# Small groups in one piece, halves crossed by ways, and another order of the first last slot: a gated-attention and mixer kernel on one core

## The chip, the cores and the metric

The kernel runs on one core of a Trainium2 chip. The metric is the time of one execution on the device in microseconds; the times quoted are of single executions or the median of several. The engines are TensorE (PE; its weight loads are PEld), VectorE (DVE), ScalarE (ACT), GpSimd (POOL) and SyncE (SP), which issues all DMAs here. Each takes its instructions in order and waits on semaphores.

## The reference, cut to what matters

Eight batches, each with 3136 positions of 256 values:

```
scores = z @ z.T / 3136;  x = u * (relu(scores)**2 @ v)      # attention, gated
h = (x.T @ U @ V).T                                          # rank 32, mixes positions
y = x + h
out = y + relu(y @ w_ch1) @ w_ch2                            # 256 -> 1024 -> 256
```

## The kernel before, in words

**Tiles.** The 3136 positions of a batch are cut into seven groups: six of 512 and a small one of 64. An item is a batch and a group; there are 56, and a slot of the main loop does the attention of one item, the (x + h) unit of the item seven slots back, the first layer (w_ch1) of the item eight back and the second layer (w_ch2) of that same item. So the small groups of batches 0 to 5 come to their first layer in the slots whose attention is of group 0 of batches 2 to 7. After the main loop come seven more slots without attention (the loop over `k` at the end of the kernel, below called the last slots): slot k does the first layer of group k of the last batch beside the second layer of the group before, and the small groups of the last two batches fall into k = 0 and k = 5. The last of these slots has a second layer only, done in two halves of 256 positions (`ch2_halves`).

**Row halves and ways.** All large matmuls use half of the array's rows (64), and `pair` issues two at a time, one for each half of the rows, into different banks of one PSUM buffer of two banks. In way 0 the upper half of the rows writes bank 0 and the lower half bank 1; in way 1 they are crossed. Both ways together give the full sum over 128 rows. A bank may be written by the other half of the rows only when the first has done with it: `post` (L168) puts a signal on GpSimd that waits for the last matmul of a way, and the first weight load of the next way waits for GpSimd. Between the two ways other work is placed where there is some. `Ways` makes the units of a long accumulation, all of one way and then all of the other.

**PSUM.** There are four such buffers. `take_ps` hands out the one that a running estimate says is free first; the matmul that first writes it waits for the engine that read its old content.

**First layer.** `ch1_part` computes two of the eight blocks of 128 hidden values for all positions of a group, in one way; `parts` lists the eight calls of an item. After way 1 the result is rectified out of PSUM into a block, by VectorE (L903) or ScalarE (L906), whichever the estimate says is free first. For a small group each call is two pairs with 64 columns, and each of its four PSUM buffers is rectified by an instruction of 128x128 elements. `by_pair` orders the calls of a small group in the last slots so that way 1 follows way 0 of the same two blocks.

**Second layer.** `ch2_stream` accumulates it over the hidden values in both ways; `ch2_out` adds (x + h) (L980) and stores. For a small group `ch2_small` (L994) uses four tiles of the array, and `four_sums` (L680, L682, L684) and L980 add up. `ch2_halves` makes two `Ways` in two PSUM buffers, one for each half; its adds are L966 and its stores L967.

**(x + h).** `u2_unit` multiplies V and t1 (t1 = x.T U, made by `t1_all`: L742, then L754, L755 and a copy to the lower rows, L756), adds x on VectorE (L815), casts the sum to bf16 (L198 on ScalarE or L200 on VectorE) and turns it by a DMA transpose (L730) into `u2T`, the input of the first layer. For group 0 of the last batch, `u2T_unit` makes the turned sum directly (L859) from an x that was turned earlier; its plain sum is made by `u2_unit` with turn=False.

**Order.** `emit` runs a list of light units (pairs of a long accumulation) and puts units from queues between them: each entry has a place (an index in the light units), the number of PSUM buffers that should be free, and the unit. The places are written by hand. Other matmuls seen in the profile are the scores (zzT; evicted by L358 on ScalarE or L354 on VectorE, squared by L348) and the attention (v_bf).

Of the kernel before, what the change touches and what calls it, by code (L numbers as in the profile page):

```python
# [10 lines left out]
AF = mybir.ActivationFunctionType  # L11
# [7 lines left out]
def kernel(  # L19
# [11 lines left out]
    nc = tc.nc  # L31
# [52 lines left out]
    def take_block():  # L84
        k = free_blocks.pop(0)
        return k, pool.tile([P, GT, GW], BF16, name=f"blk{k}", bufs=1)
# [77 lines left out]
    def post(k):  # L164

        last = [wrote[k, bank] for bank in range(2) if (k, bank) in wrote]
        if any(e[2] is None for e in last):
            x = nc.gpsimd.nop(nofuse=True)  # L168
            for e in last:
                behind(x, e[1])  # L170
                e[2] = x
# [163 lines left out]
    def flat_of(entry):  # L335
        return entry[1].rearrange("p a c -> p (a c)")
# [529 lines left out]
    def ch1_part(b, g, h0, way, box):  # L866
# [37 lines left out]
        else:  # L904
            ps_free[k] = book("act", ready, 9.5 * gw / GW)
            nc.scalar.activation(out=r, in_=ps[:, :, :gw], func=AF.Relu)  # L906

    def ch2_stream(b, g, box):
        def step(i, way, first, least):
            if first:  # L910
                box["k"], box["ps"] = take_ps()
            k, a = divmod(i, 2)
            pair(
                box["k"],
                crossed(
                    way,
                    a,
                    lambda h, q: dict(
                        out=four(box["ps"])[:, q, :],
                        lhsT=relus[b, g][k // GT][1][h, k % GT, q * P : (q + 1) * P],  # L920
                        rhs=w2_bf[h, k, :],
                        start=first,
                        stop=(least == 2 * NH and a == 1),
                    ),
                ),
                D,
            )
            if way == 0 and i == 2 * NH - 1:
                post(box["k"])
            if least == 2 * NH:  # L930
                ps_free[box["k"]] = book("dve", clock[0] + 3, 11.2)
                ch2_out(b, g, four(box["ps"]))

        return Ways(2 * NH, 0, step, box)

    def ch2_halves(b, g):

        units = []
        g0 = groups[g][0] // P
        for a in range(2):  # L940
            box = {}

            def step(i, way, first, least, a=a, box=box):
                if first:
                    box["k"], box["ps"] = take_ps()
                pair(
                    box["k"],
                    crossed(
                        way,
                        0,  # L950
                        lambda h, q: dict(
                            out=box["ps"][:, q // 2, :D],
                            lhsT=relus[b, g][i // GT][1][h, i % GT, (2 * a + q // 2) * P : (2 * a + q // 2 + 1) * P],
                            rhs=w2_bf[h, i, :],
                            start=first,
                            stop=(least == NH),
                        ),
                    ),
                    D,
                )  # L960
                if way == 0 and i == NH - 1:
                    post(box["k"])
                if least == NH:
                    ps_free[box["k"]] = book("dve", clock[0] + 3, 6.4)
                    o = u2s[b, g][:, 2 * a : 2 * a + 2, :]
                    nc.vector.tensor_tensor(out=o, in0=box["ps"][:, :, :D], in1=o, op=ALU.add)  # L966
                    nc.sync.dma_start(out=rows_of(out[b])[:, g0 + 2 * a : g0 + 2 * a + 2, :], in_=o)  # L967
                    queued(GW // 2)

            units += Ways(NH, 0, step, box).units  # L970
        return units

    def ch2_out(b, g, acc):

# [13 lines left out]
    def ch2_small(b, g):  # L988
        k, ps = take_ps()
        rows = groups[g][1]  # L990
        for kt in range(NH):
            c = kt % 2
            for h in range(2):
                nc.tensor.matmul(  # L994
                    out=ps[c * hp : c * hp + rows, h, :D],
                    lhsT=relus[b, g][kt // GT][1][h * hp : (h + 1) * hp, kt % GT, :rows],
                    rhs=w2_bf[h * hp : (h + 1) * hp, kt, :],
                    start=(kt < 2),
                    stop=(kt >= NH - 2),
                    tile_position=(h * hp, c * hp),  # L1000
                )
        pe(NH / 2 + 2)
        sums = u2s[b, g][:rows, 1:3, :]
        four_sums(k, ps, sums)
        ch2_out(b, g, sums[:, 0:1, :])
        book("dve", clock[0] + 3, 3)
# [41 lines left out]
    def parts(item, box):  # L1048

        return [  # L1050
            lambda h=h, way=way: ch1_part(*item, h, way, box)
            for h0 in range(0, NH, 4)
            for way in range(2)
            for h in (h0, h0 + 2)
        ]
# [184 lines left out]
    for t in range(n_items):  # L1240
# [60 lines left out]
        if av and full:  # L1301

            last = nA - 9
            for h, x, y in zip(hs, (4, 22, 36, 62), (16, 32, 48, last)):
                qc.append((x, 1, False, one(h, 0)))
                qc.append((y, 0 if y == 32 else 1, y != 32, lambda h=h, y=y: (scores(y != 32), one(h, 1)())))
            n = len(mine) - 3
            qs += [(9 + 74 * i / n, 1, False, lambda: scores(1)) for i in range(n)]
        elif av:

            for h, x in zip(hs, (22, 32, 42, 52)):
                qc += [(x, 1, False, one(h, 0)), (x + 8, 0, False, one(h, 1))]
            if fin:
                qc.append((72, 1, False, lambda: ch2_small(*fin)))
            k = min(2, len(mine) // 3)
            n = len(mine) - 3 * k
            at = [1 + 80 * i / n for i in range(n)]
            if t == 0:
                at = [8, 8, 26, 38, 42, 56, 64, 72, 80]
                for i, x in ((2, 22), (3, 34)):  # L1320
                    qm.append((x, 0, False, lambda i=i: z_turn(0, i * 2 * GT, on_act)))
            qs += [(x, 1, False, lambda: scores(1)) for x in at]
            qs += [(x, k, True, lambda: scores(k)) for x in (16, 48 if t else 46, nA - 2) if k]
        else:

            small = lambda: av_small(*att)
            order = mine[:1] + [small] + mine[1:]
            if mix:
                c0, c1, d0, d1, c2, c3, d2, d3 = parts(mix, box1)
                up = [lambda: u2_unit(*u2i)]  # L1330
                if fin:
                    order = [c0] + mine[:1] + [c1, d0, d1] + [c2] + mine[1:] + [c3, d2, d3] + up
                else:
                    order = up + [small, c0, c1, d0, d1, c2, c3, lambda: t1_all(att[0]), d2, d3]
            qc += [(0, 0, False, f) for f in order]
# [22 lines left out]
    def queue(places, parts):  # L1358
        return [(x, int(i % 4 < 2 and x != 16), False, f) for i, (x, f) in enumerate(zip(places, parts))]

    def by_pair(parts):
        return [parts[i] for i in (0, 2, 1, 3, 4, 6, 5, 7)]

    for k in range(NQ + 1):
        fin = (B - 1, k - 1) if k else (B - 2, NQ - 1)
        mix = (B - 1, k) if k < NQ else None
        light = ch2_halves(*fin) if k == NQ else ch2_stream(*fin, {}).units
        first, qm = parts(mix, {}) if mix else [], []
        if k == 0:
            few = by_pair(parts((B - 2, NQ), {}))  # L1370
            qc = queue((8, 10, 12, 14, 16, 18, 20, 22), few) + queue((19, 21, 24, 25, 27, 29, 31, 32), first)
            qm.append((2, 0, False, lambda: u2_unit(B - 1, 1)))
            qm.append((5, 1, False, lambda: u2T_unit(*direct)))
            qm.append((22, 1, False, lambda: u2_unit(*direct, turn=False)))
            qm.append((30, 1, False, lambda: u2_unit(B - 1, 2)))
        else:
            last = k == NQ - 1
            qc = queue((1, 2, 5, 6, 10, 11, 14, 16) if last else (1, 4, 8, 12, 16, 20, 24, 28), first)
            if k + 2 <= NQ:
                qm.append((2, 1, False, lambda: u2_unit(B - 1, k + 2)))  # L1380
            if last:
                qc += queue((17, 19, 20, 22, 24, 26, 28, 30), by_pair(parts((B - 1, NQ), {})))
            if k == 1 or k == NQ:
                qm.append((9, 1, False, lambda b=B - 2 if k == 1 else B - 1: ch2_small(b, NQ)))
        emit(light, [qc, qm])
# [30 lines left out]
```

## Time and profile before

| | |
|---|---|
| median of 3 runs | 993.44 us (992.78 to 994.03) |
| profiled execution | 993.46 us, its span 991.7 us |
| granted TensorE clock | 1.000 |
| matmuls | 16137 |
| DMA, mean over the span | 178 GB/s; 87 GB/s after 925 us |
| first layer of small groups | 256 matmuls of 64 columns; evictions 128x128: 26 on ScalarE (281 ns), 6 on VectorE (283 ns) |
| waits of weight loads for GpSimd's signals | 66, 12.5 us in all; 12 after 940 us, 2.7 us |

A line of the groups has the place in the code, the engine and operation, the tiles written and read, the shapes, and the busy time. A line of the timeline has start and length in us, engine, place, operation, tiles and count; merged instructions overlap, so the pitch of matmuls is read from starts. The chain that ended last is followed back from the end: each piece has start, length and what ran. In the list of waits a line has the engine and place that waited, for whom, the total in us, the number, and the longest.

### The profile page before, as it was taken

The numbers are of one execution on the slowest core, as the hardware profiler recorded it, in microseconds if no ns is written. First come the engines' busy times: TensorE is split into PE (matmuls) and PEld (weight loads), VectorE is DVE, ScalarE is ACT, GpSimd is POOL, SyncE is SP. The second block draws the span as 40 slices with busy tenths as digits, with TensorE's granted clock in tenths as the row PEclk, the third lists the DMA queues.
The fourth block names the chain that finished last, engine by engine and source line by source line (L and its number), as shares of the span: only waits on it lengthen the run. The fifth ranks groups of instructions, "written<-read, shape, count | busy, mean of one in ns | idle before, by whom it ended". The sixth has DMA issues, their size and how long they took to land.

```text
span 991.7 us, 35369 instructions
## 1 busy us (share of the span) xinstructions
PE 974.0 (98%) x16137; PEld 781.9 (79%) x16137; DVE 616.7 (62%) x791; ACT 492.9 (50%) x587; POOL 17.2 (2%) x24
## 2 busy tenths in 40 slices
PE   5999999999999999999999999999999999999998
PEld 3898789877778777787777877788777877787766
DVE  5977765667556675566755567555765666643453
ACT  5887742457324573355533455434653256522363
POOL 4100000000000000000000000000000000000000
PEclk9999999999999999999999999999999999999999
DMA  7999999879997799887998799975999889864142
GB/s 247 191 213 229 199 205 213 195 142 226 209 177 167 170 210 199 201 138 187 208 213 177 131 202 205 213 165 130 209 228 191 150 167 167 167 123 106 45 108 92
DMA packets 372118, 176.38 MB, mean 178 GB/s; under 512 B 347264, under 2 KB 350336, under 8 KB 371968
## 3 DMA queue, kind: packets, MB, share of 16 engines
q1 hardware_dynamic: 371968, 174.12, 86.8%
q8 instruction: 126, 2.06, 0.9%
q14 instruction: 24, 0.20, 0.1%
HBM read 62.56 MB, written 25.69 MB: 89 GB/s over the span
## 4 chain that ended last, share of the span: by engine, by line
PE 96%; DVE 1%; ACT 1%; DMA 1%; POOL 0%; issue 0%; SPq 0%; POOLq 0%; ACTq 0%
PE ps L178 94%; PE ps L661 1%; PE ps L742 1%; DMA blk<-in_v_dram 1%; DVE blk L348 1%; PE ps L994 0%; ACT blk L358 0%; ACT blk L906 0%; POOL z_bf L229 0%; DVE blk L354 0%; DVE x_bf L694 0%; PE ps L315 0%; POOL v_bf L249 0%; ACT v_bf L198 0%; ACT w_bf L198 0%
## 5 line engine op out<-in xcount | busy, mean ns | idle before, releaser
L178 PEld LDWEIGHTS <-blk 64*128 64x128 bf16 x12288 | 618.1, 94 | 148.9 <-POOLq L168 7.7
L178 PE MATMUL ps<-v_bf,blk 64*128 64x256 bf16 x9216 | 613.1, 269 | 3.6 <-DVE blk L348 1.8
L358 ACT ACTIVATE blk<-ps 128x1024 bf16<-128x1024 f32 x339 | 319.6, 974 | 365.1 <-PE ps L178 360.4
L348 DVE TENSOR_TENSOR blk<-blk 128x1024 bf16<-128x1024 bf16 x352 | 226.6, 667 | 42.7 <-ACT blk L358 42.1
L178 PE MATMUL ps<-u2T,w_bf 64*128 64x512 bf16 (+1 forms) x1792 | 237.2, 349 | 0.4
L178 PE MATMUL ps<-w_bf,blk 64*128 64x256 bf16 x3072 | 194.1, 269 | 0.6 <-ACT blk L906 0.4
L903 DVE TENSOR_SCALAR blk<-ps 128x1024 bf16<-128x1024 f32 (+1 forms) x107 | 125.3, 1171 | 89.9 <-PE ps L178 89.9
L906 ACT ACTIVATE blk<-ps 128x1024 bf16<-128x1024 f32 (+1 forms) x117 | 99.1, 857 | 90.7 <-PE ps L178 90.2
L178 PE MATMUL ps<-zzT 64*128 64x512 bf16 (+2 forms) x902 | 130.3, 329 | 1.7 <-ACT zzT L324 1.7
L178 PEld LDWEIGHTS <-w_bf 64*128 64x128 bf16 x1792 | 90.6, 94 | 29.4 <-POOLq L168 4.8
L694 DVE TENSOR_TENSOR x_bf<-ps,u_sb 128x1024 bf16<-128x1024 f32 x48 | 58.8, 1224 | 70.7 <-PE ps L178 70.6
L815 DVE TENSOR_TENSOR out_sb<-ps,x_bf 128x1024 f32<-128x1024 f32 (+1 forms) x49 | 54.2, 1107 | 59.3 <-PE ps L178 59.3
L980 DVE TENSOR_TENSOR out_sb<-ps,out_sb 128x1024 f32<-128x1024 f32 x42 | 51.3, 1222 | 18.3 <-PE ps L178 18.3
L178 PEld LDWEIGHTS <-zzT 64*128 64x128 bf16 x902 | 41.9, 95 | 7.9 <-ACT zzT L324 2.2
L178 PE MATMUL ps<-t_sb,V_bf 64*128 64x256 bf16 x200 | 20.8, 269 | 0.0
L198 ACT CAST x_bf<-out_sb 128x1024 bf16<-128x1024 f32 (+1 forms) x21 | 17.4, 826 | 6.0 <-DVE out_sb L815 6.0
L200 DVE CAST v_bf<-stage 128x1024 bf16<-128x1024 f32 (+1 forms) x33 | 20.2, 612 | 0.0
L178 PE MATMUL ps<-v_bf,last_sb 64*128 64x256 bf16 x192 | 18.6, 269 | 0.0
L354 DVE TENSOR_SCALAR blk<-ps 128x1024 bf16<-128x1024 f32 (+1 forms) x9 | 10.0, 1106 | 13.0 <-PE ps L178 13.0
L682 DVE TENSOR_TENSOR u_sb<-ps,u_sb 64x512 f32<-64x512 f32 x8 | 5.5, 683 | 17.1 <-ACT u_sb L680 17.1
L198 ACT CAST v_bf<-stage 128x1024 bf16<-128x1024 f32 x15 | 15.6, 1041 | 0.0
L980 DVE TENSOR_TENSOR blk<-ps,blk 128x1024 f32<-128x1024 f32 x5 | 6.1, 1225 | 14.2 <-PE ps L178 14.2
(68 smaller groups left out, 229.0 us busy)
## 6 DMA issues: line engine op xcount, KB each, us to landing
u_sb<-in_u_dram SPq DMA_DIRECT2D x48, 512.0 KB, 5.0
stage<-in_v_dram SPq DMA_DIRECT2D x42, 512.0 KB, 6.3
out_dram<-out_sb SPq DMA_DIRECT2D x42, 512.0 KB, 3.1
stage<-in_z_dram SPq DMA_DIRECT2D x7, 512.0 KB, 6.0
blk<-in_v_dram SPq DMA_DIRECT2D x6, 512.0 KB, 7.0
out_dram<-blk SPq DMA_DIRECT2D x5, 512.0 KB, 2.7
blk<-blk SPq DMA_TRANSPOSE x156, 5.3
blk<-in_moe_w_ch_dram SPq DMA_DIRECT2D x4, 512.0 KB, 5.5
```

Source lines behind the costliest of these rows:

```text
L178: ins = nc.tensor.matmul(**args)
L198: nc.scalar.copy(out=out, in_=in_)
L200: nc.vector.tensor_copy(out=out, in_=in_)
L348: nc.vector.tensor_tensor(out=a, in0=a, in1=a, op=ALU.mult)
L354: nc.vector.tensor_scalar(out=dst, in0=src, scalar1=scale, scalar2=0.0, op0=ALU.mult, op1=ALU.max)
L358: nc.scalar.activation(out=dst, in_=src, func=AF.Relu, scale=scale)
L661: nc.tensor.matmul(out=ps[c * hp : c * hp + rows, h, :D], lhsT=smalls[b][h * hp : (h + 1) * hp, place_of(jt), :], rhs=v_bfs[b][h * hp : (h ...
L694: nc.vector.tensor_tensor(out=xs[b, g][:rows, :n, :], in0=four(box["ps"])[:rows, :n, :], in1=u_sbs[b, g][:rows, :n, :], op=ALU.mult,)
L815: nc.vector.tensor_tensor(out=o[:rows, :n, :], in0=four(ps)[:rows, :n, :], in1=x, op=ALU.add)
L903: nc.vector.tensor_single_scalar(out=r, in_=ps[:, :, :gw], scalar=0.0, op=ALU.max)
L906: nc.scalar.activation(out=r, in_=ps[:, :, :gw], func=AF.Relu)
L980: nc.vector.tensor_tensor(out=o, in0=acc, in1=o, op=ALU.add)
```

## The change

Three edits.

1. The first layer of a small group is no longer four pairs of calls but one piece of two calls (`ch1_small`), one for each way, of eight pairs each. All eight blocks of hidden values of the 64 positions go into one PSUM buffer (four blocks to a bank), with one signal between the ways and one eviction of 128x512 elements into one block instead of two. `ch2_small` reads its weights from there. In the six slots of the main loop the calls stand at places 36 and 48, in the last slots at 13 and 19 (k = 0) and 18 and 23 (k = 5).
2. `ch2_halves` returns its units by ways: way 0 of the first half, way 0 of the second, way 1 of the first, way 1 of the second.
3. In the last slot k = 0 the direct unit of group 0 (`u2T_unit`) comes before the (x + h) unit of group 1, and the places of the four units and of group 0's first layer are new.

```diff
+    def small_relu(b, g):
+        return flat_of(relus[b, g][0])[:, : NH * groups[g][1]]
+
+    def ch1_small(b, g, way, box):
+        gw = groups[g][1]
+        while (b, g) not in u2Ts:
+            run_held(min(h[0] for h in held))
+        if way == 0:
+            relus[b, g] = [take_block()]
+            box["k"], box["ps"] = take_ps()
+        k, ps = box["k"], box["ps"]
+        for n in range(NH // 2):
+            for db in range(ND):
+                ops = []
+                for h in range(2):
+                    bank = h if way == 0 else 1 - h
+                    ht = 2 * n + bank
+                    ops.append(
+                        (
+                            h,
+                            bank,
+                            dict(
+                                out=ps[:, bank, n * gw : (n + 1) * gw],
+                                lhsT=w1_bf[h * hp : (h + 1) * hp, db, ht * P : (ht + 1) * P],
+                                rhs=u2Ts[b, g][h * hp : (h + 1) * hp, 0, db, :gw],
+                                start=(way == 0 and n == 0 and db == 0),
+                                stop=(way == 1 and n == NH // 2 - 1 and db == ND - 1),
+                            ),
+                        )
+                    )
+                pair(k, ops, gw)
+        if way == 0:
+            post(k)
+            return
+        r = small_relu(b, g).rearrange("p (n j c) -> p j n c", j=2, c=gw)
+        src = ps[:, :, : NH // 2 * gw].rearrange("p j (n c) -> p j n c", c=gw)
+        ready = clock[0] + 3
+        if max(free_at["dve"], ready) + 1 < max(free_at["act"], ready):
+            ps_free[k] = book("dve", ready, 6.4)
+            nc.vector.tensor_single_scalar(out=r, in_=src, scalar=0.0, op=ALU.max)
+        else:
+            ps_free[k] = book("act", ready, 5.4)
+            nc.scalar.activation(out=r, in_=src, func=AF.Relu)
...
-            units += Ways(NH, 0, step, box).units
-        return units
+            units.append(Ways(NH, 0, step, box).units)
+        return [f for way in range(2) for u in units for f in u[way * NH : (way + 1) * NH]]
...
-                    lhsT=relus[b, g][kt // GT][1][h * hp : (h + 1) * hp, kt % GT, :rows],
+                    lhsT=small_relu(b, g)[h * hp : (h + 1) * hp, kt * rows : (kt + 1) * rows],
...
-            for h, x in zip(hs, (22, 32, 42, 52)):
-                qc += [(x, 1, False, one(h, 0)), (x + 8, 0, False, one(h, 1))]
+            if mix:
+                qc += [(x, 1 - way, False, lambda way=way: ch1_small(*mix, way, box1)) for way, x in ((0, 36), (1, 48))]
...
-    def by_pair(parts):
-        return [parts[i] for i in (0, 2, 1, 3, 4, 6, 5, 7)]
+    def small_parts(item, places):
+        box = {}
+        return [(x, 1 - way, False, lambda way=way: ch1_small(*item, way, box)) for way, x in enumerate(places)]
...
-            few = by_pair(parts((B - 2, NQ), {}))
-            qc = queue((8, 10, 12, 14, 16, 18, 20, 22), few) + queue((19, 21, 24, 25, 27, 29, 31, 32), first)
-            qm.append((2, 0, False, lambda: u2_unit(B - 1, 1)))
-            qm.append((5, 1, False, lambda: u2T_unit(*direct)))
-            qm.append((22, 1, False, lambda: u2_unit(*direct, turn=False)))
-            qm.append((30, 1, False, lambda: u2_unit(B - 1, 2)))
+            qc = small_parts((B - 2, NQ), (13, 19)) + queue((16, 18, 20, 21, 24, 26, 28, 30), first)
+            qm.append((3, 0, False, lambda: u2T_unit(*direct)))
+            qm.append((9, 1, False, lambda: u2_unit(B - 1, 1)))
+            qm.append((17, 1, False, lambda: u2_unit(*direct, turn=False)))
+            qm.append((25, 1, False, lambda: u2_unit(B - 1, 2)))
...
-                qc += queue((17, 19, 20, 22, 24, 26, 28, 30), by_pair(parts((B - 1, NQ), {})))
+                qc += small_parts((B - 1, NQ), (18, 23))
```

## The prediction

> **What bounds the kernel.** I read the shares of the page first, then the chain that ended last.
>
> ```profile
> PE 974.0 (98%) x16137; PEld 781.9 (79%) x16137; DVE 616.7 (62%) x791; ACT 492.9 (50%) x587; POOL 17.2 (2%) x24
> ...
> PE 96%; DVE 1%; ACT 1%; DMA 1%; POOL 0%; issue 0%; SPq 0%; POOLq 0%; ACTq 0%
> ```
>
> TensorE bounds it. The change keeps every matmul, so it can only pay where TensorE waits. Next the timeline of a slot with a small group (the first of six, 120.1 us apart), and of a burst of small score matmuls:
>
> ```profile
> 201.71 0.53 PE L178 MATMUL ps<-zzT 64*128 64x64 bf16 x24
> ...
> 202.06 0.19 PE L542 MATMUL ps<-zzT 64*128 64x64 bf16 x1
> ...
> 224.82 0.22 PE L178 MATMUL ps<-u2T,w_bf 64*128 64x64 bf16 x4
> ...
> 224.88 0.93 PE L178 MATMUL ps<-v_bf,blk 64*128 64x256 bf16 x14
> ...
> 225.64 0.38 PE L178 MATMUL ps<-t_sb,V_bf 64*128 64x256 bf16 x4
> ```
>
> The pitch of a pair (the two row halves run together) is read from the starts: seven pairs of 256 columns in 0.76 us, 0.109 each; two of 64 columns in 0.06, and twelve in 0.35, 0.029 each. A 512-column pair takes 0.216 (227.34 to 227.56). By these pitches TensorE loses nothing between 224.82 and 231.82, and the waits of its weight loads there are a single one, of the second layer:
>
> ```profile
> PEld L994 <- issue: 0.2, 1, 0.2
> ```
>
> So the six slots have nothing to give. The end has. Its chain, in two windows:
>
> ```profile
> 935.52 0.02 ACTq L906
> 935.54 0.04 issue
> 935.59 1.95 ACT blk L906 x2
> 937.53 0.04 issue
> 937.58 0.91 PE ps L178 x22
> 938.49 0.02 issue
> 938.51 0.03 POOLq L168
> ...
> 944.45 1.03 ACT blk L906
> 945.48 0.04 issue
> 945.52 0.48 PE ps L178 x5
> ```
>
> ```profile
> 980.99 0.03 POOLq L168
> ...
> 981.83 0.03 POOLq L168
> ...
> 983.89 0.03 POOLq L168
> ...
> 986.60 0.03 POOLq L168
> ...
> 986.67 1.07 PE ps L178 x16
> 987.73 0.02 issue
> 987.75 0.69 DVE blk L966
> ```
>
> Every `POOLq L168` is a turn of ways: TensorE finishes the last matmul of one way (0.27 us where the pitch is 0.109), GpSimd passes it on, and only then comes the next load. Start against pitch, one turn costs 0.28 to 0.29 us. `ACT L906` in the chain is a PSUM buffer that TensorE waits for.
>
> **Part 1: small groups in one piece.** Per group the 32 matmuls (16 pairs, 0.46 us) stay; three of four turns, three of four evictions and one of two blocks go. In the six slots the turns were covered by 0.4 us or more of attention matmuls, so TensorE gains 0. ScalarE loses its evictions of 0.28 each and, by the new order, one score eviction of 1.03; it gets one of 128x512 as four runs of 64 columns. No row shows that form; between 0.28 (128x128) and 1.02 (128x1024) I take 0.60, the 594 and 607 ns of other 128x512 evictions. VectorE loses one of 0.28 and gets that score eviction at 1.22; its squares come later. What hides this: it has caught up by 232.3, before the sums of the second layer (L682, 233.2). PSUM releases, walked through the slot: the tightest is the second-last score pair, asked for at 228.88 from a buffer that ScalarE frees at 228.77 (1.02 after 227.75), 0.06 to spare once the 0.05 of a hand-over is taken off. GpSimd has only these signals here, in the order TensorE needs them, and SyncE's order is unchanged. Net 0; if that cover fails, see the third rival.
>
> The last small group lies in the open: from 979.95 to its second layer at 984.18 TensorE loses 0.28 + 0.28 + 0.07 at three turns of small pieces, 0.03 in restarts, and 0.28 at the turn of the last group's first half. Of these 0.94 I leave 0.04: in the new order 5 pairs (0.55 us) stand between the two ways of the small piece. Gain **0.90**.
>
> **A rule against it.** The sixteen matmuls now stand in one burst, with a weight load each. The mean load is 94 ns, a pair's pitch 29; a burst of twelve pairs of this very shape (zzT above) holds 29, so I leave the pitch. The Trainium skill (TensorE: Matmul & The Clock Gate, "Back-to-back issue gap") says that in a stream of loads and matmuls both set the spacing, and gives about 81 ns per matmul at 128 columns; by that, an estimate, sixteen bursts of sixteen would cost 16 x (1.30 - 0.23) = 17 us more, and the trace does not agree.
>
> **Part 2: the first of the last slots, reordered.** From 935.75 the pairs are the same in both: 38 of 256 columns (4.14), 17 of 512 (3.67), 16 of 64 (0.46): 8.27, so 944.03 without waits. Before, the next slot begins at 945.52: 1.49 lost (0.26 at 937.58 for L906, 0.29 at 938.58 for a turn, 0.18 at 939.05 for a small eviction, 0.52 at 945.52 for L906, the rest in five pieces up to 0.10).
> The new order, walked with the same pitches:
> - the direct (x + h) unit (u2T_unit) is third; the lower copy of t1 ends 936.06, +0.05: 0.04 lost. VectorE adds it (L859) 936.52 to 937.74, where the transposed unit's add (L815) stood; L815 follows to 938.98, its cast (L198) to 940.06, its transpose (L730) leaves SyncE 1.2 us later than before.
> - second-layer weights from the second L906 (ends 937.53): asked for at 937.53, had at 937.59: 0.06 lost.
> - small piece, way 0, at 937.70, way 1 at 939.68; eviction 940.10 to 940.70; its buffer is next asked for at 940.88. Covered by 0.13; above 0.73 for the eviction each ns counts.
> - first-layer buffers are asked for at 939.25 (free 939.03), 941.86 (941.77), 942.40 (942.23): no loss.
> - the next slot's accumulator, at 944.14, takes the buffer of an eviction that can only start at 943.45 and takes 1.02: 944.53, 0.39 lost.
> Lost 0.49: gain **1.00**.
> Then the second slot gives some back. VectorE now has half of the first-layer evictions (1.22 each). Group 1's second half asks at 948.22 for a buffer that ScalarE gets at 947.43 and frees at 948.45: 0.28 lost, where this slot lost nothing at that place before. VectorE's releases (945.16, 946.30, 947.44, 949.14, 950.30) come 0.01 to 0.24 before they are asked for. Back **0.28**, at most 0.5. Net of part 2: **0.72**.
> Two transposes follow behind: group 1's lands at 940.08 + 4.6 = 944.7 (4.6 is the longest of the seven issues of L730 after 925 us, and is this one's), needed 945.18; group 2's stands in SyncE's queue behind the store of L980, which VectorE finishes 0.4 later than before; needed 952.7, there by 952.0.
>
> **Part 3: the halves interleaved by ways.** Between the ways of a half now lie eight pairs of the other, 0.87 us, against 0.28 lost: both turns vanish; the first is in the 0.90 above, the second is after the second layer of the small group. At the end TensorE is then no longer last: the sums of that group (L680, L682, L684, L980) hold VectorE until 2.88 after its first matmul (984.18 to 987.06), then come the two halves' adds of 0.68 and 0.69, overlapping by 0.08. The last add ended 4.27 after that matmul (988.45) and will at 4.10; the store waits for it as before (988.47), and SyncE is free at 4.11. So of the second turn's 0.28 only **0.14** reaches the end.
>
> **Sum.** 0.90 + 0.72 + 0.14 = 1.76 us off this execution's 993.46: 991.70. The median of the runs is 993.44, so 991.7 for it too. About 0.2% (1.99 us, below 991.45) is what a measurement of this kernel tells from no change: the forecast lies just on the near side.
>
> **Rivals.**
> 1. More: the two new ScalarE waits (0.39 + 0.28) do not come. For it: two evictions in a row take 1.95, not 2.04. Against: each starts on an idle engine when TensorE ends. 991.0; chance 0.18.
> 2. Less: a transpose is late. For it: L730 took up to 7.0 us elsewhere; group 1's would then land at 947.1, 1.9 after it is needed. Against: that was under full DMA load; the mean is 87 GB/s after 925 us against 178 overall. 993.6 at worst, 992.5 at half of it; chance 0.10.
> 3. Slower: the six slots. VectorE's extra 1.22 makes TensorE wait for a buffer in each. It cancels the gain at 0.29 per slot and shows as slower from 0.63; at a whole eviction, 6 x 1.22 = 7.3, so 999.0. For it: the release with 0.06 to spare. Against: VectorE and ScalarE were busy 5.8 and 6.0 of these 7.0 us; VectorE's share grows by 0.94 and ScalarE's falls. Chance 0.06.
> 4. Slower: the bursts bind on loads, 8 x 0.094 against 0.23, +0.52 in 16 bursts: 8.3, so 1000.0. Against: the twelve pairs. Chance 0.04.
>
> That the change does not do what it says is no rival: the new instruction order has the bursts and the crossed halves.
>
> **Numbers.** The forecast keeps 0.62. Its own doubt (0.5 for the second slot's waits, 0.4 for the eviction's length) puts about 4 in 10 of it past 991.45: 0.25, and with rival 1 faster has 0.43. Same: 0.37 + 0.10. Slower: 0.10. The range: 990.7 is all 2.7 us of the end's waits (1.49 + 0.94 + 0.28) gone, 993.4 is all of the gain given back; outside lie rivals 3 and 4 and the worst of 2.
>
> **What would show it.** The 64-column matmuls of the six slots in two groups of sixteen at 29 ns a pair, and no new wait there; two weight-load waits on GpSimd fewer around 981 and none at 984 and 986.7; the slots of the end beginning near 944.5 and 952.65 instead of 945.52 and 953.37; one ACT wait of 0.3 to 0.4 at each of 944 and 948; the last store 1.8 earlier. I am wrong if the six slots shift against the run before, if the second slot loses over 0.5, or if the accumulators begin later than that.

## The result, and the profile after

The changed kernel takes 991.79 us, the median of 12 runs (989.56 to 992.82), beside 993.63 us for twelve runs of the kernel before (991.08 to 995.69): a ratio of 0.9984 on record, with a 95% interval of 0.9976 to 0.9992 (the two medians alone give 0.9981). The interval ends below 1, so the gain is clear of noise, but it is a gain of 0.08 to 0.24%. The profiled execution took 992.52 us, its span is 990.7.

Single executions of one kernel differ by 3 to 5 us, and even the start of the last slots lies between 934.1 and 937.6 us in the profiles used here. So most of what follows is read from **the last slots** alone: from the first matmul of their second layer to the end of the last add on VectorE. That is 52.69 us before (935.75 to 988.45) and 51.23 after (936.08 to 987.31). The changed kernel gains **1.46 us** there. Its profiled execution starts this stretch 0.33 later than the one before, which has to be taken off before times of the two are compared.

The page first, shares and chain:

```profile
PE 972.5 (98%) x16137; PEld 782.3 (79%) x16137; DVE 624.2 (63%) x794; ACT 483.5 (49%) x560; POOL 17.1 (2%) x24
...
PE 96%; DMA 1%; DVE 1%; ACT 1%; POOL 0%; issue 0%; SPq 0%; DVEq 0%
```

The same bound, the same number of matmuls. ScalarE lost 27 instructions and 9.4 us, VectorE gained 3 and 7.5 us. The timeline of the first slot with a small group (start, length, engine, place, operation, shapes, count):

```profile
226.89 0.40 PE L178 MATMUL ps<-u2T,w_bf 64*128 64x64 bf16 x16
227.12 0.71 PE L178 MATMUL ps<-v_bf,blk 64*128 64x256 bf16 x10
...
228.65 0.40 PE L178 MATMUL ps<-u2T,w_bf 64*128 64x64 bf16 x16
228.88 0.27 PE L178 MATMUL ps<-v_bf,blk 64*128 64x256 bf16 x2
...
229.09 0.60 ACT L952 ACTIVATE blk<-ps 128x512 bf16<-128x512 f32 x1
```

Eight pairs from 226.89 to 227.12 and again from 228.65 to 228.88: 0.23 each, 29 ns a pair, so a burst of sixteen matmuls, each with its own weight load, runs at the pitch that the prediction took from the small score matmuls. The eviction takes 0.60. The starts of the small second layer of the six slots lie 120.10 us apart, as before.

The chain of the last slots:

```profile
943.79 1.03 ACT blk L906
944.83 0.04 issue
944.87 2.90 PE ps L178 x38
947.77 0.02 issue
947.80 0.45 ACT blk L906
948.25 5.16 DMA u2T<-x_bf
953.41 0.05 issue
953.45 29.84 PE ps L178 x437
983.30 0.59 PE ps L1040 x16
983.89 0.02 issue
983.91 0.59 ACT blk L680
...
985.70 0.42 DVE blk L1026
986.11 0.60 DVE blk L1012
986.71 0.60 DVEq L1457
```

No `POOLq L168` is left in it. Two things took its place: the sums of the small group on VectorE at the very end, which was expected, and `948.25 5.16 DMA u2T<-x_bf`, which was not. This is the transpose (L730) of group 2's (x + h). Who waits for it stands in the waits of the first three last slots (engine, place, for whom, total, number, longest); the wait for L906 in the second line is that of the second slot's accumulator at 944.87:

```profile
PEld L178 <- DMA u2T<-x_bf: 0.4, 1, 0.4
...
PE ps L178 <- ACT blk L906: 0.2, 1, 0.2
```

A second wait for L906 leaves too short an idle time for that list and is read from starts. Six light matmuls (three pairs) begin at 948.23, so the next pair could start at 948.56; it starts at 948.87, when the eviction that began at 947.80 has freed its buffer:

```profile
947.80 1.02 ACT L906 ACTIVATE blk<-ps 128x1024 bf16<-128x1024 f32 x1
...
948.23 0.51 PE L178 MATMUL ps<-w_bf,blk 64*128 64x256 bf16 x6
...
948.87 0.61 PE L178 MATMUL ps<-u2T,w_bf 64*128 64x512 bf16 x4
```

### The profile page after: what moved, and what is told of

The parts are those of the page before. It is cut to its first block, busy times and chain, and to the rows that moved or that the text cites. A ratio compares the mean times of both kernels' runs of the same rounds, so it can differ in the third digit from the quotient of the medians.

```text
span 990.7 us, 35313 instructions
## 1 busy us (share of the span) xinstructions
PE 972.5 (98%) x16137; PEld 782.3 (79%) x16137; DVE 624.2 (63%) x794; ACT 483.5 (49%) x560; POOL 17.1 (2%) x24
## 4 chain that ended last, share of the span: by engine, by line
PE 96%; DMA 1%; DVE 1%; ACT 1%; POOL 0%; issue 0%; SPq 0%; DVEq 0%
PE ps L178 93%; PE ps L661 1%; PE ps L742 1%; DMA blk<-in_v_dram 1%; DVE blk L348 1%; DMA u2T<-x_bf 1%; PE ps L1040 0%; ACT blk L358 0%; POOL z_bf L229 0%; DVE blk L354 0%; ACT blk L906 0%; POOL v_bf L249 0%; DVE x_bf L694 0%; PE ps L315 0%; ACT v_bf L198 0%
## 5 line engine op out<-in xcount | busy, mean ns | idle before, releaser
L358 ACT ACTIVATE blk<-ps 128x1024 bf16<-128x1024 f32 (+1 forms) x333 | 314.7, 974 | 375.8 <-PE ps L178 374.2
L348 DVE TENSOR_TENSOR blk<-blk 128x1024 bf16<-128x1024 bf16 x352 | 224.1, 664 | 36.1 <-ACT blk L358 35.6
L178 PE MATMUL ps<-u2T,w_bf 64*128 64x512 bf16 (+1 forms) x1792 | 228.9, 349 | 0.3 <-DMA u2T<-x_bf 0.2
L903 DVE TENSOR_SCALAR blk<-ps 128x1024 bf16<-128x1024 f32 x105 | 128.5, 1224 | 93.3 <-PE ps L178 93.3
L906 ACT ACTIVATE blk<-ps 128x1024 bf16<-128x1024 f32 x87 | 88.4, 1023 | 81.8 <-PE ps L178 81.3
L178 PEld LDWEIGHTS <-w_bf 64*128 64x128 bf16 x1792 | 84.5, 94 | 27.4 <-POOLq L168 4.1
L354 DVE TENSOR_SCALAR blk<-ps 128x1024 bf16<-128x1024 f32 (+1 forms) x15 | 17.3, 1154 | 19.5 <-PE ps L178 19.5
L200 DVE CAST x_bf<-out_sb 128x1024 bf16<-128x1024 f32 x21 | 14.5, 689 | 0.3
```

Source lines behind the costliest of these rows:

```text
L178: ins = nc.tensor.matmul(**args)
L200: nc.vector.tensor_copy(out=out, in_=in_)
L348: nc.vector.tensor_tensor(out=a, in0=a, in1=a, op=ALU.mult)
L354: nc.vector.tensor_scalar(out=dst, in0=src, scalar1=scale, scalar2=0.0, op0=ALU.mult, op1=ALU.max)
L358: nc.scalar.activation(out=dst, in_=src, func=AF.Relu, scale=scale)
L903: nc.vector.tensor_single_scalar(out=r, in_=ps[:, :, :gw], scalar=0.0, op=ALU.max)
```

## The ledger of the last slots

Both kernels have the same matmuls, so those with the same number counted from the end can be compared. With the 0.33 taken off, the changed kernel is ahead by this much (us):

| point | ahead | step | predicted | measured |
|---|---|---|---|---|
| first matmul of the last slots | 0 | | | |
| accumulator of the second slot | 0.98 | first slot, reordered | +1.00 | +0.98 |
| before group 2's first layer | 0.67 | buffer wait in the second slot | -0.28 | -0.31 |
| after it | 0.34 | transpose of group 2 | 0 | **-0.33** |
| second layer of the last small group | 1.28 | turns around 981 | +0.90 | +0.94 |
| end of the last add | 1.46 | end behind that layer (4.27 before, 4.08 after) | +0.14 | +0.19 |

Four of the five steps came within 0.05 us; the fifth, the transpose, stood in the prediction with nothing to lose.

**Theories.** Main theory: turns and waits pay where nothing covers them, so all of the gain is in the last slots, by these steps; and the transpose lost 0.33 because of something in its flight. Rivals: the six main slots contribute through the lighter ScalarE; the second turn of the halves gives its whole 0.28; the reorder, not the pieces, makes the first slot faster; the late transpose is chance.

## Experiments: one part at a time

Each of these was run once with a profile; the length of the last slots is what is read.

**Crossed halves alone**, on the kernel before:

```diff
-            units += Ways(NH, 0, step, box).units
-        return units
+            units.append(Ways(NH, 0, step, box).units)
+        return [f for way in range(2) for u in units for f in u[way * NH : (way + 1) * NH]]
```

> Only the crossed halves, on the kernel before. The end piece (first matmul of the last slots to the end of the last add) is 52.70 us before and 51.23 in the changed kernel. Theory (turns that come uncovered, by their place): the turn of the first half lies ahead of the small group's second layer and gives 0.28; the second turn vanishes too, but that group's sums hold VectorE, so the last add ends 4.10 us after the first matmul of the small second layer instead of 4.27: 0.14 to 0.19. End piece 52.24 to 52.30. Rival A (both turns reach the end): 52.14 and 3.99 after that matmul. Rival B (nothing behind the sums counts): 52.42 and 4.27 after it.

Measured: 52.22 us. TensorE is level with the kernel before up to the small second layer, which starts 0.29 earlier; the last add ends 4.08 after it instead of 4.27. So 0.29 + 0.19: the first turn pays in full, the second in part. TensorE itself ends 0.57 earlier, which is both turns; 0.10 of it does not arrive. Rivals A and B, at 52.14 and 52.42, are out; the theory's range began at 52.24.

**Small groups in one piece alone**: the changed kernel with the halves not crossed and the units of the first last slot in the old order.

```diff
-            qm.append((3, 0, False, lambda: u2T_unit(*direct)))
-            qm.append((9, 1, False, lambda: u2_unit(B - 1, 1)))
...
+            qm.append((2, 0, False, lambda: u2_unit(B - 1, 1)))
+            qm.append((5, 1, False, lambda: u2T_unit(*direct)))
```

> The small groups in one piece at the new places, but the halves not crossed and the (x + h) units of the first last slot in the old order. Theory: in the slot with the small group of the last batch 0.62 of the turns and restarts go (0.94 less the 0.28 of the half's turn and 0.04); in the first last slot the turn and the small eviction that were waited for (0.29 and 0.18) go and the waits for L906 (0.26 and 0.52) stay, so 0.47 there; the second slot loses nothing new and the transpose of group 2 lands 4.0 to 4.6 after its issue, in time. End piece 52.70 - 1.09 = 51.6. Rival (the order of the units is what gives the first slot its gain): that slot stays as before, 52.1.

Measured: 52.42 us, a gain of 0.27 where 1.09 was expected. The slot with the last small group gave 0.65, where 0.62 was expected. The first two slots went wrong; the chain shows it:

```profile
937.47 1.22 DVE u2T L859
938.69 0.04 issue
938.74 5.19 PE ps L178 x76
...
948.40 5.20 DMA u2T<-x_bf
```

Group 0's first layer now stands at place 16 instead of 19, and in the old order its input (L859) is only there at 938.69: TensorE loses 0.52. Of the first slot's gain 0.30 is left; the second slot's wait for a buffer (0.31) and the late transpose (0.37) take more than that back. Fifteen of the transpose's sixteen parts land 3.52 to 3.69 after its issue here, the last one after 5.20.

**The new order alone**, on the kernel before:

```diff
-            qm.append((2, 0, False, lambda: u2_unit(B - 1, 1)))
-            qm.append((5, 1, False, lambda: u2T_unit(*direct)))
-            qm.append((22, 1, False, lambda: u2_unit(*direct, turn=False)))
-            qm.append((30, 1, False, lambda: u2_unit(B - 1, 2)))
+            qm.append((3, 0, False, lambda: u2T_unit(*direct)))
+            qm.append((9, 1, False, lambda: u2_unit(B - 1, 1)))
+            qm.append((17, 1, False, lambda: u2_unit(*direct, turn=False)))
+            qm.append((25, 1, False, lambda: u2_unit(B - 1, 2)))
```

> Only the new order and places of the four (x + h) units, with the small groups in four pieces at their old places and the halves not crossed. Theory: the first last slot gains the waits for L906 only, about 0.5 of the 1.09 measured; the second slot loses 0.2 to 0.3 for a buffer; group 2's transpose is issued behind the store of the second layer and lands about 5.2 after its issue, so 0.2 to 0.3 more is lost. End piece 52.70 +- 0.2. Rival 1 (the order gives all of the first slot's gain): 52.0. Rival 2 (that the transpose came late in the changed kernel was chance): it lands 4.0 to 4.6 after its issue and nothing is lost there, 52.4.

Measured: 53.72 us, **slower** by 1.03; neither the expected figure nor a rival's. The second slot begins 0.61 ahead and the third is still 0.59 ahead; 0.55 of that goes inside the third, and then 1.07 in one piece, at group 3's first layer:

```profile
957.80 0.24 ACT blk L906
958.04 5.44 DMA u2T<-x_bf
963.48 0.05 issue
963.53 6.57 PE ps L178 x87
```

SyncE's own timeline says why the transpose is issued so late:

```profile
957.61 0.34 SPq L982 DMA_DIRECT2D out_dram<-blk  x1
958.04 4.89 SPq L730 DMA_TRANSPOSE u2T<-x_bf  x2
```

The cast that it needs was done at 954.64. With four small pieces in the slot, a buffer for group 2's unit came later, group 3's unit fell behind too, and in SyncE's order its transpose now stands behind the store of a second layer that ends only at 957.58. The late issue alone does not make the 1.07, though. TensorE asked at 962.46 (one pitch behind the last pair, at 962.35), and fifteen of the transpose's sixteen parts had landed by 961.86; the last one landed at 963.48, with a packet of TensorE's code at 961.46 in its flight (see the late transpose below). With all parts there by 961.86, the last slots would have taken 52.65, an estimate (53.72 less 1.07), level with the kernel before and inside the expected 52.70 +- 0.2.

So the parts are not gains that add. With the waits for such transposes taken off (1.07 here, 0.37 in the run before, 0.33 in the changed kernel), the order alone gives 0.04, the pieces alone 0.64 and the crossed halves 0.47, together 1.15, where the changed kernel gives 1.79; this sum is an estimate.

**The last slots alone**: the six main slots keep their four pieces and four evictions.

```diff
...
-            if mix:
-                qc += [(x, 1 - way, False, lambda way=way: ch1_small(*mix, way, box1)) for way, x in ((0, 36), (1, 48))]
+            for h, x in zip(hs, (22, 32, 42, 52)):
+                qc += [(x, 1, False, one(h, 0)), (x + 8, 0, False, one(h, 1))]
```

> The change without its part in the six main slots: there the small groups keep their four pieces and four evictions. Theory (those slots have nothing to give): everything as in the changed kernel, a period of 120.10 us between the first two such slots, end piece 51.2, time within the scatter of the changed kernel. Rival (the lighter ScalarE pays in the main loop): the stretch from 222 to 343 us 0.05 or more longer, the time 0.3 or more longer. The last slots are the changed kernel's instruction for instruction: if the late transpose of group 2 comes from its place behind the store, it lands again 5.0 to 5.3 after its issue and costs 0.3; if that was chance, 4.0 to 4.6 and nothing, and the end piece is 50.9.

Measured: 51.26 us in the last slots and 992.20 in all. Four of the five periods between the six slots are 120.10; the fourth is 120.40, and the chain names a transpose of 4.92 us at 591.25 there. So the lighter main slots give nothing on their own. And group 2's transpose lands 5.03 to 5.19 after its issue again, at a cost of 0.36, with the same instructions in the last slots: not chance.

**How wide the cover of the six slots is**: the one eviction of a small piece done twice there.

```diff
             nc.scalar.activation(out=r, in_=src, func=AF.Relu)
+            if b < B - 2:
+                nc.scalar.activation(out=r, in_=src, func=AF.Relu)
```

> The changed kernel with the one eviction of a small group's first layer done twice in the six main slots (0.60 more of ScalarE each), to find how wide the cover there is. Theory (the buffer that TensorE asks for at 230.73 is the one of the score eviction just behind, free 0.13 before): that eviction comes 0.6 to 0.7 later, so TensorE waits 0.5 to 0.6 in each of the six slots, 3 to 3.6 us in all, and the period of 120.10 us stays. Rival (the buffer asked for is the small piece's own, free 1.0 before): up to 0.1 per slot, 0 to 0.6 in all.

Measured: the periods stay at 120.10 (120.097 to 120.100), no new wait of TensorE. ScalarE's timeline has the second eviction and the score eviction behind it:

```profile
228.38 0.60 ACT L952 ACTIVATE blk<-ps 128x512 bf16<-128x512 f32 x1
229.01 0.60 ACT L954 ACTIVATE blk<-ps 128x512 bf16<-128x512 f32 x1
229.50 1.97 ACT L358 ACTIVATE blk<-ps 128x1024 bf16<-128x1024 f32 x2
```

The score eviction starts 0.63 later than in the changed kernel, and nobody asks for its buffer in that time. The pair that starts at 230.73 in the changed kernel starts at 230.02 here, before that score eviction has ended (230.52), so its buffer is not that one: the theory is out, the rival's figure is right, and the cover behind the small eviction is wider than 0.6 us. The release that the prediction gave 0.06 to spare is another one, ahead of the small eviction, and this run does not move it: in the changed kernel the score eviction ahead of the small one ends at 229.12 and the pair that needs its buffer starts at 229.21, without a wait.

**The end**: the second layer of the last small group at place 2 of the last slot instead of 9.

```diff
-                qm.append((9, 1, False, lambda b=B - 2 if k == 1 else B - 1: ch2_small(b, NQ)))
+                qm.append((9 if k == 1 else 2, 1, False, lambda b=B - 2 if k == 1 else B - 1: ch2_small(b, NQ)))
```

> The changed kernel with the second layer of the last small group seven places earlier in the last slot (place 2 instead of 9), about 0.76 us. Theory (that group's sums on VectorE hold the end: L680, L682, L684, L1026 until 2.88 after its first matmul, then the two halves' adds): the sums now end before the first half is ready, the last add starts 0.02 to 0.05 after TensorE's last matmul instead of 0.17, so the last slots end 0.13 to 0.15 earlier, with TensorE's last matmul unmoved: 51.09 us from first matmul to last add's end if the transpose of group 2 is as late as in the changed kernel (51.23). Rival (the last add follows TensorE, the sums do not matter): 51.23 as before.

Measured: 51.16 us, with TensorE's last matmul at 50.15 after the start (50.13 in the changed kernel). The timeline's adds:

```profile
983.39 0.42 DVE L1026 TENSOR_TENSOR blk<-blk 64x256 f32<-64x256 f32 x1
984.11 0.69 DVE L1012 TENSOR_TENSOR blk<-ps,blk 128x512 f32<-128x512 f32 x1 [0.29 <-PE ps L178]
...
984.98 0.69 DVE L1012 TENSOR_TENSOR blk<-ps,blk 128x512 f32<-128x512 f32 x1 [0.18 <-PE ps L178]
```

Both halves' adds now wait for TensorE, in brackets, where in the changed kernel the chain went through the sums. Measured from the last matmul's start the end comes 0.10 earlier (1.00 against 1.11): the place is right, the size a little less than the 0.13 to 0.15 expected. The last add starts 0.04 after TensorE's last matmul ends, where it was 0.17, and takes 0.69 instead of 0.67.

## Experiments: the late transpose

The records of single packets in the trace of the changed kernel show a 16 KB packet of the queue `q8 instruction` at 950.95, in the middle of the transpose's flight. Twenty of its 256-byte packets, started at 951.14 to 951.26, take 1.4 to 1.6 us; the median of such packets in the whole trace is 18 ns. In the kernel before, the transpose was issued 0.69 earlier (947.55) and its last packet had started at 950.92; the code packet came at 950.95 as well, no 256-byte packet took over 0.1 us, and the transpose landed 3.67 to 4.00 after its issue. (A transpose here has 1024 packets and reports its landing in sixteen parts; two numbers are the first part and the last.)

That queue carries TensorE's code: 126 packets of 16 KB for 32,274 matmuls and weight loads, one for 256 instructions; the run below with 256 more instructions has 127. The Trainium skill (Runtime: NRT & Kernel Launch, "Instruction fetch mechanics") says that code is refilled in blocks of 16 KiB, 256 instructions, by a DMA queue of the engine itself, and that this is mostly hidden; the block agrees with this count, "mostly hidden" is what is in question here.

**The store behind the transpose** on SyncE:

```diff
+        def store():
+            nc.sync.dma_start(out=dst, in_=o)
+            queued(n * rows)
+        if (b, g) == (B - 2, NQ - 1):
+            late.append(store)
+            return
+        store()
...
             x_turn(b, g, u2Ts[b, g])
+            if (b, g) == (B - 1, 2):
+                late.pop()()
```

> The changed kernel with the store of the second layer of the first last slot issued behind group 2's transpose instead of ahead of it; nothing else moves. In the changed kernel the transpose is issued 0.58 after the cast that it needs, 0.50 of it behind the store; it lands 5.16 later, 0.32 too late. In its flight TensorE's code is fetched (a 16 KB packet at 950.95), and 20 of its 256-byte packets, issued 0.2 to 0.3 after that, take 1.4 to 1.6 us instead of a median of 18 ns. Theory 1 (it collides with the fetch because it starts late): issued about 0.4 to 0.5 earlier and with nothing ahead in the queues, its packets are through before the fetch; it lands 3.0 to 4.0 after its issue, TensorE does not wait, and the last slots take 50.9. Theory 2 (it is as long as it is whatever stands before it): 5.0 to 5.2, landing 0.4 to 0.5 earlier, 50.9 as well or 51.0. Theory 3 (the store is what delays it, and the fetch does nothing): as theory 1. Told apart from theory 1 by the next run but one.

Measured: 50.90 us. The transpose lands 2.94 to 3.11 after its issue and TensorE does not wait. Now the store is in flight when the code packet comes: fifteen of its sixteen parts land within 2.9 us, one after 4.9, and nobody waits for that.

**The same code, moved**: 40 extra matmuls of 16 columns ahead of the first transposes of z, and in another run 128.

```diff
+        if t0 == 0:
+            for i in range(40):
+                nc.tensor.matmul(out=pz[:32, 0, :16], lhsT=ident[:, :32], rhs=ident[:, :16], start=True, stop=True)
```

> The changed kernel with 40 extra matmuls of 16 columns (80 instructions with their loads) ahead of the very first transposes of z, where TensorE waits; their result is overwritten. All work and every order behind them is the same, but TensorE's code is fetched 80 instructions, about 2.5 us, earlier against the work. Theory 1 (the late transpose of group 2 is a collision with the fetch): no fetch between its issue and its landing; it lands at most 4.1 after its issue though the store still stands ahead of it, TensorE does not wait for it, and the last slots take 50.9. Theory 3 (the store ahead of it delays it): 5.0 to 5.2 after its issue and 51.23 again.

> As the run with 40 extra matmuls ahead of the first transposes of z, but 128 of them: 256 instructions with their loads. TensorE's code is fetched in packets of 16 KB, 126 in the changed kernel for 32,274 matmuls and loads, so one for each 256 instructions. Theory 1 (collision with the fetch): the code is moved by one packet exactly, so a fetch falls again some 14.9 us after the first matmul of the last slots, as in the changed kernel; group 2's transpose lands 5.0 to 5.2 after its issue and the last slots take 51.2. Rival (any added code, or the delay at the start, is what mended the run with 40): it lands 3.4 to 4.1 after its issue and the last slots take 50.9.

Measured with 40: 50.90 us; the code packet comes 10.5 us after the start of the last slots instead of 14.9 (4.4 earlier, where about 2.5 was expected), and the transpose lands 3.45 to 3.61 after its issue. With 128: 51.25 us; the code packet is back at 14.9, 15 packets of 256 bytes hang for 1.4 to 1.5 us, and the transpose lands 5.03 to 5.18 after its issue. The DMA view of the 5.3 us from the transpose's issue shows it, first the changed kernel, then the runs with 40 and with 128 (the mean busy share of the 16 DMA engines in tenths, in 40 slices of 0.13 us; then a queue with its packets, MB and share):

```profile
DMA  0048999996799569999999990000000002500000
...
q8 instruction: 1, 0.02, 1.1%
```

```profile
DMA  0019999993999859999999960000000000000000
...
q1 hardware_dynamic: 1200, 0.79, 54.5%
```

```profile
DMA  0009999994999849999999990000010000200000
...
q8 instruction: 1, 0.02, 1.1%
```

The store and the transpose keep the engines busy for about the same time in all three. With a code packet in the window, a last bit of work follows (`25`, `2`) before the transpose counts as done; without one (only q1 moved anything) it ends where the nines end.

In all three the store stands ahead of the transpose, with 0.50 us between their issues. So it is the code packet that costs the 0.33, and the store only puts the transpose in its way. Extra instructions as such mend nothing, since 128 bring the loss back.

The long packets are not what every late transpose has in common. The packet records of group 2's transpose in eight of the runs say this (times in us after its issue; the store is the one issued 0.5 ahead):

| run | store ahead | code packet | 256-byte packets started behind it | of them 0.9 or more behind | packets over 1 us | landed |
|---|---|---|---|---|---|---|
| changed kernel | yes | 2.71 | 296 | 106 | 20 | 5.01 to 5.16 |
| 128 extra matmuls | yes | 2.77 | 264 | 44 | 15 | 5.03 to 5.18 |
| last slots alone | yes | 2.88 | 155 | 25 | 0 | 5.03 to 5.19 |
| one piece alone | yes | 3.18 | 3 | 3 | 0 | 3.52 to 5.20 |
| kernel before | yes | 3.40 | 0 | 0 | 0 | 3.67 to 4.00 |
| 40 extra matmuls | yes | none | | | 0 | 3.45 to 3.61 |
| store behind | no | 3.24 | 0 | 0 | 0 | 2.94 to 3.11 |
| both mends (below) | no | 2.56 | 0 | 0 | 0 | 2.91 to 3.14 |

The runs with the double eviction and with the early second layer are like the last slots alone (code packet at 2.81 and 2.82, no packet over 1 us, landed by 5.17 and 5.19). What the late ones share is that some of their packets start only 0.9 us or more behind the start of the code packet, which itself takes 0.93 to 0.96; the last part then lands 2.0 to 2.5 us behind that start. Where the transpose's packets have all started before the code packet, it is on time here. That border is not sharp: in the run with the new order alone group 2's last packet starts 0.01 ahead of the code packet, and one of the sixteen parts still lands 2.02 behind it.

## Experiments: better versions

**Both mends together**: the store behind the transpose and the small second layer at place 2.

> The changed kernel with both mends: the store of the first last slot behind group 2's transpose, and the second layer of the last small group at place 2 of the last slot. They act at different places, so the sum of what each gave alone: 51.23 - 0.33 - 0.10 = 50.80 us from the first matmul of the last slots to the last add's end, 1.9 less than before (52.69). Time 0.9981 of before or a little less, with the interval below 1. Rival (the two share a wait): 50.9.

Measured: 50.80 us in the last slots, as expected; 990.31 us (median of 9 runs) beside 993.22 (16 runs of the kernel before), a ratio of 0.9975 with an interval of 0.9964 to 0.9985.

**And the third pair of blocks of group 0 earlier:**

```diff
-            qc = small_parts((B - 2, NQ), (13, 19)) + queue((16, 18, 20, 21, 24, 26, 28, 30), first)
+            qc = small_parts((B - 2, NQ), (13, 19)) + queue((16, 18, 20, 21), first[:4])
+            qc += [(26, 0, False, f) for f in first[4:]]
...
-            qm.append((25, 1, False, lambda: u2_unit(B - 1, 2)))
+            qm.append((26, 1, False, lambda: u2_unit(B - 1, 2)))
```

> As the kernel with both mends, and the last four calls of group 0's first layer at place 26 of the first last slot without waiting for a free buffer in the estimate (before: from place 29 on). In the changed kernel the next slot's accumulator waits 0.42 us for an eviction of the third pair of blocks. Theory (that wait comes from the calls being late, not from a lack of buffers): the third pair starts 0.3 to 0.4 earlier, at the release of the first pair's buffer, its eviction ends before the next slot asks, and the 0.42 go: 50.4. Rival (the buffers are all taken: the wait moves to the calls themselves, or to the second slot, which lost 0.25 for one): 50.7 to 51.0.

Measured: 50.68 us, and 989.66 us (median of 7 runs), a ratio of 0.9971 with an interval of 0.9959 to 0.9982. The wait of 0.42 at the second slot's accumulator is gone, but the calls themselves wait: they begin 0.14 after the pair ahead of them is done, and their eight pairs take 1.87 instead of 1.73 us. So 0.12 is gained of 0.42: the rival is right, at a length just under its 50.7 to 51.0. The two calls start at 940.81 and 941.39, each 0.05 after an eviction has ended (940.76 on ScalarE, 941.34 on VectorE): their buffers were still in use. By the last slots this is the fastest version, 2.02 us ahead of the kernel before and 0.55 ahead of the changed one.

## Why the prediction was right, and where not

- **The total.** Forecast 991.7, measured 991.79; forecast gain 1.76, measured in the traces 1.46. The medians differ by 1.84, so the agreement of the total to 0.1 us is partly luck: the executions scatter by more than the 0.30 that was missing.
- **First slot, reordered (+1.00).** Right, 0.98. The wait that it named, 0.39 for an eviction on ScalarE ahead of the second slot's accumulator, was 0.42, at 944.54 with the offset taken off (predicted 944.53). The walk by pitches held. But it is a gain of order and pieces together: the order alone gave 0.61 there, the pieces alone 0.30, and in the two slots behind it both lost more than that, with 1.07 and 0.37 of the loss at a transpose that a code packet made late.
- **Second slot (-0.28).** Right, 0.31, all of it the wait for ScalarE's eviction that ends at 948.82: asked for at 948.23 by the clock of before (predicted 948.22), had at 948.54.
- **Group 2's transpose ("needed 952.7, there by 952.0").** The step that failed: it landed at 953.1 by the clock of before. Need and issue were right (947.92, predicted 0.4 later than 947.55); the flight was taken to be no longer than the 4.0 us of before, and it was 5.16, because a code packet now fell among its packets: the transpose was issued 0.37 later in the slots, and the code packet came 0.33 earlier in them. The rival of a late transpose was in the prediction, with its price up to 1.9 and a chance of 0.10, but for group 1's and by load on the DMA engines; it was group 2's, at light load.
- **The last small group (+0.90).** Right, 0.94. The bursts of sixteen hold 29 ns a pair. So the figure of the Trainium skill (TensorE: Matmul & The Clock Gate, "Back-to-back issue gap"), 81 ns per matmul at 128 columns, does not carry over to these pairs of 64 columns on row halves.
- **The second turn (+0.14).** Right in kind, a little small: the halves alone gave 0.19 behind the small second layer where the turn is worth 0.28, and moving that layer ahead gave 0.10 more. The prediction's own ends, 4.27 before and 4.10 after, make 0.17 and not 0.14.
- **The six slots (0).** Right, shown by the run with the last slots alone and by the periods of 120.10. The release with 0.06 to spare held, with 0.09 from the eviction's end to the pair's start, hand-over included. The rivals of slower slots and of bursts bound by loads are out.
- **Rival 1 (the ScalarE waits do not come).** Both came.

## What to carry to other kernels

A step that removes waits is worth what is uncovered at its own place, and matching matmuls by their number in two traces shows place by place what arrived. When an order is shifted by half a microsecond, the DMAs that move with it need a price of their own, from the longest flights in the trace and not from the last one: what they meet in flight changes. Where a transpose feeds the next matmul, issue it ahead of a store that nobody waits for: here that took the last slots from 51.23 to 50.90 us.

## What the runs showed of the hardware

A transpose whose packets meet a packet of TensorE's code lands late. With a store issued 0.5 us ahead, the same transpose took 3.61 us without a code packet in its flight and 5.16 to 5.20 with one among its packets. Moving the code by 80 instructions took the loss away, moving it by 256 brought it back. In the main loop this is mostly covered, but not always: in the run with the new order alone TensorE lost 1.50 us at 718.46 to a transpose with a code packet at 716.16, and in the run with the crossed halves alone 0.34 at 597.36, with a code packet at 595.31. These account for 1.51 and 0.36 us by which the last slots of those two profiles start later; whether they explain the scatter between executions of one kernel is not shown.

Often small packets hang as well. In the trace of the changed kernel 1,112 packets of 256 bytes take 1.2 us or more; 67% of them start 0.1 to 0.7 us after a 16 KB code packet, where only 5% of all such packets start. Behind 75 code packets 256-byte packets start in that stretch, and behind 57 of them at least one hangs. But three of the runs with a transpose landing at 5.17 to 5.19 have no hanging packet in it, so the hang is a companion of the delay and not its cause in all of them. What happens in the engines the traces do not show.
